# Joined score tiles, softmax steps for two heads at once, and earlier chunk additions in a kernel of attention and MLP

## The chip, the core and the metric

The kernel runs on one core of one Trainium2 chip. The metric is the device time of one execution in microseconds (us); lower is better. Three runs of the kernel before gave 613.06, 613.56 (the median) and 614.54 us. The profile shown here is of another execution, which took 613.01 us.

A core has these engines: TensorE (PE, matrix products; its weight loads are listed as PEld), VectorE (DVE, elementwise arithmetic), ScalarE (ACT, activation functions and copies), GpSimd (POOL), and SyncE (SP), which here only issues DMAs. Each has its own queue of instructions and runs it in order. They wait for each other with semaphores.

## The reference

Causal attention over 4 batches of 12 heads, 448 tokens and 64 features a head, and behind it an MLP on the 1792 tokens with 768 features, 2048 hidden features and a leaky ReLU:

```
scores = scale * q @ k.T                 # per batch and head, 448 x 448
scores = where(mask, -1e9, scores)       # mask: triu(k=1), causal
scores = scores - max(scores, axis=-1)
attn   = exp(scores); attn = attn / (sum(attn, axis=-1) + 1e-9)
x      = attn @ v                        # heads side by side: 1792 x 768
h      = x @ w_in                        # 768 x 2048
out    = maximum(0.01 * h, h) @ w_out    # 2048 x 768
```

q, k and v are float32. The two weight matrices come as float64 and are read as pairs of 32-bit words.

## The kernel before

**Units.** Two heads of one batch make a unit; there are 24, u = 0 to 23, six to a batch. A unit's scores lie with the keys on the 128 partitions and the queries on the columns, in four chunks of 128 keys. Since the mask is causal, chunk c needs only the queries from 128c on: 448, 320, 192 and 64 columns. Chunks 3 and 0 of a head fill one PSUM bank, chunks 2 and 1 a second, so a unit takes four banks. Four banks have the names S0 to S3; up to unit 7 the two banks of layer 1 (mm0, mm1) serve as well, so that a unit and a half have room.

**Steps of a unit** (lines of before):
- `features`: PE transposes k and q (L375), ACT copies them out (kq, L378).
- `scores`: 16 matmuls (L404) and eight small ones that add the mask (L418); in the text "S".
- `head`, for each of the two heads: ACT copies chunk 0 into M (L433); DVE takes the maximum of M and chunks 1, 2, 3, three instructions (L435 to 437, shown by the profile at the helper's line L236); POOL reduces M over the partitions (L438, result MR); DVE subtracts MR from the chunks, four instructions of 64, 448, 192 and 320 columns into t (L443); ACT takes exp of t (L450).
- `products`: 16 matmuls t by v (L462), which ACT copies out as xu (L468).
- `finish`, after each second unit: PE sums t over the keys for four heads with a matrix of ones (L482). In batches 0 and 1 all four chunks are summed, 32 matmuls. In batches 2 and 3 DVE first adds the chunks onto each other (`add`, L488 to 492, three instructions a head) and PE sums one chunk, 8 matmuls. ACT copies the sums out (sr, L494); a DMA spreads them, DVE takes the reciprocal (L497, L498), DMAs store and broadcast it (rb), DVE divides (L512), and x is split into a rounded part (x hi, ACT, L513) and the rest (x lo, DVE, L514).

**Weights.** `weights_in` unpacks w_in in 16 pieces: one ACT and three DVE instructions make a float32 of the words (L316 to L322), ACT rounds it into wh (L337), DVE takes the rest, wl (L340). The stage tile for it shares its memory with x of batches 1 and 3.

**MLP.** `layer1` multiplies x by a piece for one batch: 18 matmuls make one h tile (L536), 64 tiles, 1152 matmuls. ACT applies the leaky ReLU (L542) and SP writes the tile to DRAM. `weights_out` and `layer2` follow, with 1176 matmuls at L723.

**What sets the order.** `Plan` collects the instructions with a planned duration and a due time, and then lists them one by one: the engine that is free first takes, of its instructions that are ready at that time by the plan, the one with the smallest due time (L105 to 109). A step's due time is the unit's number plus an entry of the table LATER (`turn`, L207). The pieces of weights have PIECE[0] + PIECE[1] * f (L746), layer 1 numbers far behind (L767 to 769), so its matmuls fill what attention leaves free; SAME favours a PE instruction of the same kind as the last. The list is then the program order on every engine; on the chip, an engine waits in that order.

**Memory.** M and MR have two tiles each, t six (NTB), one per head.

Of the kernel before, what the change touches and what calls it, by code (L numbers as in the profile page):

```python
# [8 lines left out]
F32 = mybir.dt.float32  # L9
# [11 lines left out]
    "add": 89.39, "load": -27.59, "v": 46.78, "transpose": 57.39, "features": 318.14, "scores": 12.88,  # L21
    "chunk 0": 37.99, "max": -23.03, "all max": -55.97, "subtract": -12.57, "exp": 18.88, "products": 35.62,
    "take products": 0, "sums": -9.93, "take sums": -52.68, "spread": -20.75, "invert": 56.94, "store": -44.79,
    "broadcast": 373.59, "divide": 13.16, "x hi": -28.06, "x lo": 62.49,
}

EARLY = 8

PIECE = (97.36, -5.57)


SAME = 25.68
# [115 lines left out]
def attention_moe_kernel(  # L148
# [52 lines left out]
    for j in range(2):  # L201
        P.slot["mm", ("S", 4 + j)] = j
# [51 lines left out]
    place = p1.tile([128, S], F32, tag="M0", name="place")[:, 0:128]  # L254
# [9 lines left out]

    big = [pp.tile([128, 512], F32, tag=f"big{i}", name="big") for i in range(2)]
# [6 lines left out]
    memset(lambda: place[:, 0:1], 0.0, (), [("M", 0)], FIRST)  # L272
    for i in range(7):
        n = 2 ** i
        dve(n, lambda n=n: nc.vector.tensor_scalar(out=place[:, n:2 * n], in0=place[:, 0:n], scalar1=float(n), scalar2=None, op0=ALU.add),
            (), [("M", 0)], FIRST)
    pe(0.3, lambda: nc.tensor.matmul(out=at_row, lhsT=place[0:1, :], rhs=ones[0:1, 0:1], start=True, stop=True), [("M", 0), "ones"], ["at_row"], FIRST)
    dve(1, lambda: nc.vector.tensor_copy(out=row, in_=at_row), ["at_row"], ["row"], FIRST)
    def table(out_, n, col, key, **how):
        dve(n, lambda: nc.vector.tensor_scalar(out=out_, in0=place[:, 0:n], scalar1=col, **how), ["row", "rows", ("M", 0)], [key], FIRST)  # L280
# [102 lines left out]
    order = sorted(segs)  # L383

    def scores(u):

        kq = ("kq", u % 2)


        sl = [2 * ((2 * u + bank) % 3 if u < EARLY else bank) + e for e in range(2) for bank in range(2)]  # L390
        S_ = ("S", u)

        def f(banks):
            for bank in banks:
                for e in range(2):
                    j = sl[2 * e + bank]
                    T[S_, 2 * e + bank] = (mm if j > 3 else pp).tile([128, 512], F32, tag=f"mm{j - 4}" if j > 3 else f"S{j}", name="S")
            for bank in banks:
                cs = [c for c in order if segs[c][2] == bank]
                for c in cs:  # L400
                    qs, n, _, col = segs[c]
                    for e in range(2):
                        rows = slice(64 * e, 64 * e + 64)
                        nc.tensor.matmul(out=T[S_, 2 * e + bank][:, col:col + n], lhsT=T[kq][rows, 128 * c:128 * c + 128],  # L404
                                         rhs=T[kq][rows, S + qs:2 * S], start=c == cs[0], stop=False)

            for i, w in enumerate((first, last_)):
                for bank in banks:
                    for e in range(2):
                        rows = slice(64 * e, 64 * e + 64)  # L410
                        o = T[S_, 2 * e + bank]
# [8 lines left out]
        for banks in ((0,), (1,)) if u <= EARLY else ((0, 1),):  # L420
            pe(1.17 * len(banks), lambda banks=banks: f(banks), [kq, (*kq, 0), (*kq, 1), "maskb"], [("S", sl[2 * e + bank]) for bank in banks for e in range(2)],
               turn("scores", u), rows=120, cfg=1)
        for e in range(2):
            head(2 * u + e, e, sl)

    def head(g, e, sl):

        u = g // 2
        S_ = ("S", u)
        m, mr, t = ("M", g % 2), ("MR", g % 2), ("t", g % NTB)  # L430
        bk = lambda c: ("S", sl[2 * e + segs[c][2]])
        s = lambda c: T[S_, 2 * e + segs[c][2]][:, segs[c][3]:segs[c][3] + segs[c][1]]
        act(S + 55, both(new(m, p1, [128, S], F32, f"M{g % 2}"), lambda: nc.scalar.activation(out=T[m], in_=s(0), func=ACTF.Copy)),  # L433
            (), [m, bk(0)], turn("chunk 0", u))
        for c in order[1:]:  # L435
            qs, n, _, _ = segs[c]
            tt(lambda qs=qs: T[m][:, qs:], lambda c=c: s(c), lambda qs=qs: T[m][:, qs:], ALU.max, n, (), [m, bk(c)], turn("max", u), chain=0.02)
# [369 lines left out]
```

## Time and profile before

| | |
|---|---|
| median of 3 runs | 613.56 us (613.06 to 614.54) |
| profiled execution | 613.01 us, of which the span of the trace is 611.1 us |
| PE busy | 597.0 us, 98% of the span |
| DVE busy | 446.9 us, 73% |
| ACT busy | 292.1 us, 48% |
| POOL busy | 82.2 us, 13% |
| TensorE clock granted | 1.00, the upper of its two levels (2.4 GHz) |

"Busy" counts the time in which an engine executes. In a timeline, neighbouring instructions of one kind are drawn together with their count (x4), and the text names the shape of the first; the time in brackets at the end is idle time in front of the row, with the engine whose signal ended it. A shape 128x448 is partitions by columns. The steps of weights and attention fill the trace up to 263 us; the last quarter of layer 1 and layer 2 follow.

### The profile page before, as it was taken

Reading aid. Unit: us, or ns where it says so; the run is one execution under the profiler, and the core shown is the slowest. Engines: PE = TensorE matmul, PEld = TensorE weight load, DVE = VectorE, ACT = ScalarE, POOL = GpSimd, SP = SyncE. Lnnn points to the kernel's source line nnn. Section 1 sums busy time; section 2 is a strip of 40 time slices with the busy share of each in tenths; the row PEclk is TensorE's granted clock in tenths of the full one; section 3 lists DMA queues with packets and bytes.
Section 4 is the critical chain, followed back from the end, with each engine's and each line's share of the span. In section 5 each row is a group of like instructions: output and inputs, shape, how many; then the busy total and the mean of one; then the engine's idle time right before and its main releaser. Section 6 shows DMA issues by size and latency. Waiting matters only on the chain.

```text
span 611.1 us, 10491 instructions
## 1 busy us (share of the span) xinstructions
PE 597.0 (98%) x3850; PEld 517.7 (85%) x3850; DVE 446.9 (73%) x935; ACT 292.1 (48%) x499; POOL 82.2 (13%) x54
## 2 busy tenths in 40 slices
PE   8889999999999999999999999999999999999997
PEld 6656666779867677789999999999999999999997
DVE  3899998999579778711466799778857676767655
ACT  3767766666555554512333555545333233323231
POOL 1545332332024234200000000000000000000000
PEclk9999999999999999999999999999999999999999
DMA  8987977855474433112588764113523333333201
GB/s 166 240 175 158 194 195 165 240 166 164 124 165 113 118 106 81 43 57 88 196 274 276 276 209 131 62 47 103 156 70 121 89 117 110 99 95 96 70 30 39
DMA packets 130466, 82.90 MB, mean 136 GB/s; under 512 B 72560, under 2 KB 128368, under 8 KB 130416
## 3 DMA queue, kind: packets, MB, share of 16 engines
q1 hardware_dynamic: 126576, 76.74, 44.6%
q10 hardware_dynamic: 3840, 5.51, 3.4%
q8 instruction: 30, 0.49, 0.3%
q14 instruction: 20, 0.16, 0.1%
HBM read 61.87 MB, written 20.27 MB: 134 GB/s over the span
## 4 chain that ended last, share of the span: by engine, by line
PE 74%; DVE 14%; DMA 4%; issue 3%; ACT 3%; POOL 3%; SPq 0%; ACTq 0%; POOLq 0%; DVEq 0%
PE h L723 31%; PE h L536 30%; PE S L404 4%; PE big L462 4%; DVE t L443 3%; DVE M L236 3%; POOL MR L438 3%; PE big L375 2%; PE big L482 2%; DMA rb<-scr 1%; DVE wl L340 1%; DVE stage L319 1%; DVE stage L321 1%; DMA stage<-in_moe_w_in_dram 1%; DMA kraw<-in_k_dram 1%
## 5 line engine op out<-in xcount | busy, mean ns | idle before, releaser
L536 PE MATMUL h<-xt,wh 128*128 128x448 f32 x768 | 222.7, 371 | 0.0
L723 PE MATMUL h<-W,r 128*128 128x384 f32 x882 | 164.1, 334 | 0.1
L723 PEld LDWEIGHTS h<-W,r 128*128 128x128 f32 x882 | 153.7, 188 | 0.7 <-DVE r L589 0.4
L536 PEld LDWEIGHTS h<-xt,wh 128*128 128x128 f32 x768 | 141.6, 188 | 13.8 <-issue 0.7
L536 PE MATMUL h<-xt,wl 128*128 128x448 f32 x384 | 140.9, 367 | 0.0
L438 POOL PARTITION_ALL_REDUCE MR<-M x48 | 81.7, 1747 | 171.5 <-DVE M L236 136.8
L536 PEld LDWEIGHTS h<-xt,wl 128*128 128x128 f32 x384 | 72.1, 188 | 6.7
L588 ACT ACTIVATE r<-v 128x512 fp32r<-128x512 f32 x70 | 41.9, 599 | 71.8 <-DVE v L586 71.7
L542 ACT ACTIVATE h<-h 128x448 f32<-128x448 f32 x64 | 34.7, 542 | 76.6 <-PE h L536 49.6
L443 DVE TENSOR_TENSOR t<-S,MR 128x64 f32<-128x64 f32 x192 | 67.5, 413 | 4.9 <-POOL MR L438 4.7
L589 DVE TENSOR_TENSOR r<-v,r 128x512 fp32r<-128x512 f32 x70 | 47.3, 690 | 28.4 <-ACT r L588 26.6
L236 DVE TENSOR_TENSOR M<-S,M 128x320 f32<-128x320 f32 x144 | 49.1, 354 | 20.7 <-ACT M L433 9.6
L723 PE MATMUL h<-xw,r 128*128 128x384 f32 x294 | 61.9, 334 | 0.0
L450 ACT ACTIVATE t<-t 128x1024 f32<-128x1024 f32 x48 | 50.7, 1057 | 21.2 <-DVE t L443 17.0
L404 PE MATMUL S<-kq 64*128 64x448 f32 (+3 forms) x384 | 57.0, 412 | 0.1
L723 PEld LDWEIGHTS h<-xw,r 128*128 128x128 f32 x294 | 51.9, 188 | 0.0
L404 PEld LDWEIGHTS S<-kq 64*128 64x128 f32 x384 | 36.1, 191 | 18.7 <-issue 13.4
L586 DVE TENSOR_TENSOR v<-A 128x512 f32<-128x512 f32 (+1 forms) x71 | 47.7, 689 | 0.0
L462 PE MATMUL big<-t,v 128*64 128x448 f32 (+3 forms) x384 | 46.6, 386 | 0.1
L462 PEld LDWEIGHTS big<-t,v 128*64 128x64 f32 x384 | 25.4, 136 | 21.9 <-issue 11.4
L433 ACT ACTIVATE M<-S 128x448 f32<-128x448 f32 x48 | 24.3, 539 | 23.4 <-POOL MR L438 11.8
L588 ACT ACTIVATE r<-A 128x512 fp32r<-128x512 f32 x28 | 17.7, 632 | 30.8 <-PE h L723 30.7
(84 smaller groups left out, 525.4 us busy)
## 6 DMA issues: line engine op xcount, KB each, us to landing
gd<-h SPq DMA_DIRECT2D x64, 224.0 KB, 2.3
A<-gd SPq DMA_DIRECT2D x28, 512.0 KB, 3.7
stage<-in_moe_w_in_dram SPq DMA_DIRECT2D x16, 768.0 KB, 5.8
A<-in_moe_w_out_dram SPq DMA_DIRECT2D x16, 768.0 KB, 5.7
kraw<-in_k_dram SPq DMA_DIRECT2D x24, 224.0 KB, 3.8
qraw<-in_q_dram SPq DMA_DIRECT2D x24, 224.0 KB, 4.3
rb<-scr ACTq DMA_DIRECT2D x48, 112.0 KB, 3.1
v<-in_v_dram SPq DMA_DIRECT2D x48, 96.0 KB, 3.2
```

Source lines behind the costliest of these rows:

```text
L236: return dve(n, lambda: nc.vector.tensor_tensor(out=out_(), in0=a(), in1=b(), op=op), r, w, prio, **kw)
L404: nc.tensor.matmul(out=T[S_, 2 * e + bank][:, col:col + n], lhsT=T[kq][rows, 128 * c:128 * c + 128], rhs=T[kq][rows, S + qs:2 * S], start= ...
L438: P.op("Pool", 1.75, both(new(mr, p1, [128, S], F32, f"MR{g % 2}"), lambda: nc.gpsimd.partition_all_reduce(T[mr], T[m], 128, ReduceOp.max) ...
L443: f = lambda c=c, qs=qs, n=n: nc.vector.tensor_tensor(out=T[t][:, at(c):at(c) + n], in0=s(c), in1=T[mr][:, qs:], op=ALU.subtract)
L450: act(1024 + 55, lambda: nc.scalar.activation(out=T[t], in_=T[t], func=ACTF.Exp, scale=scale), (), [t], turn("exp", u))
L462: nc.tensor.matmul(out=bigs(key[1])[64 * e:64 * e + 64, qs:S], lhsT=T[vv][:, c, e, :], rhs=T["t", (2 * u + e) % NTB][:, 512 * bank + col:5 ...
L536: nc.tensor.matmul(out=T[key][:, :S], lhsT=T[w, f, 1][:, 128 * c:128 * c + 128], rhs=T["xt", b][:, x, :], start=(c == 0 and j == 0), stop= ...
L542: lambda key=key, g=g: nc.scalar.activation(out=T[g], in_=T[key][:, :S], func=ACTF.Prelu, alpha=0.01)),
L586: nc.vector.tensor_tensor(out=x(), in0=get(terms[0]), in1=get(terms[1]), op=ALU.add if terms[2] > 0 else ALU.subtract)
L588: act(n, lambda: nc.scalar.activation(out=hi(), in_=x(), func=ACTF.Copy), [*rd, *hold], [(out_cell, "h")], prio)
L589: return dve(n, lambda: nc.vector.tensor_tensor(out=lo(), in0=x(), in1=hi().bitcast(F32), op=ALU.subtract), [*rd, (out_cell, "h")], [out_c ...
L723: nc.tensor.matmul(out=T[key][:, :HO], lhsT=g()[:, jj * 128:jj * 128 + 128], rhs=W[:, w * HO:(w + 1) * HO], start=(e == 0 and jj == 0 and ...
```

## The change

Five things are changed:

1. A unit's score banks are joined in pairs: the two heads' banks of one kind make one tile of two banks, [128, 2, 512]. There are two such tiles, SS, apart from layer 1's two banks, which serve as the third pair up to unit 7.
2. M, MR and t become tiles for both heads, with two tiles of M, one of MR and three of t. MR and t keep their size so, and M's memory doubles.
3. One instruction may then do a step for both heads. The copy of chunk 0 does so wherever the bank pair is a joined tile (all units but 1, 4 and 7); maxima and subtractions do so from unit 8, the ninth, on. The all-reduce stays one for each head, and so does exp.
4. Chunk additions (and so 8 matmuls of sums in place of 32) begin at batch 1 instead of batch 2, each instruction for both heads of a unit.
5. The tables LATER, PIECE and SAME have new numbers, and the all-reduce's planned duration is 1.52 instead of 1.75. The constants at the start use rb0's memory instead of M0's.

```diff
 LATER = {
-    "add": 89.39, "load": -27.59, "v": 46.78, "transpose": 57.39, "features": 318.14, "scores": 12.88,
+    "add": 62.28, "load": -49.69, "v": 26.95, "transpose": 115.6, "features": -54.79, "scores": -10.32,
...
-PIECE = (97.36, -5.57)
+PIECE = (260.59, -34.81)
-SAME = 25.68
+SAME = -28.38
...
+    SS = [pp.tile([128, 2, 512], F32, tag=f"S{i}", name="S") for i in range(2)]
...
+    NTB, NM = 3, 2
+    ADDS = 1
+    MERGE = [lambda u: u >= 0, lambda u: u >= 8, lambda u: u >= 8]
+    for tag, n, width_ in (("M", NM, S), ("MR", 1, S), ("t", NTB, 1024)):
+        for i in range(n):
+            T[tag, i] = p1.tile([128, 2, width_], F32, name=f"{tag}{i}")
...
-        sl = [2 * ((2 * u + bank) % 3 if u < EARLY else bank) + e for e in range(2) for bank in range(2)]
+        sl = [(2 * u + bank) % 3 if u < EARLY else bank for bank in range(2)]
...
+                    T["S", u, bank, e] = SS[sl[bank]][:, e] if sl[bank] < 2 else mm.tile([128, 512], F32, tag=f"mm{e}", name="S")
...
+        heads = lambda merged: [(0, 1)] if merged else [(0,), (1,)]
...
+        for es in heads(MERGE[0](u) and sl[0] < 2):
+            act(len(es) * S + 55, lambda es=es: nc.scalar.activation(out=T[m][:, cut(es)], in_=s(0, es), func=ACTF.Copy),
+                (), cells(m, es) + bk(0, es), turn("chunk 0", u))
+        for es in heads(MERGE[1](u) and max(sl) < 2):
+            for c in order[1:]:
+                qs, n, _, _ = segs[c]
+                tt(lambda qs=qs, es=es: T[m][:, cut(es), qs:], lambda c=c, es=es: s(c, es), lambda qs=qs, es=es: T[m][:, cut(es), qs:], ALU.max, len(es) * n,
+                   (), cells(m, es) + bk(c, es), turn("max", u), chain=0.02)
         for e in range(2):
...
+            P.op("Pool", 1.52, lambda e=e: nc.gpsimd.partition_all_reduce(T[mr][:, e], T[m][:, e], 128, ReduceOp.max),
+                 [(*m, e)], [(*mr, e)], turn("all max", u))
...
+        for es in heads(MERGE[2](u) and max(sl) < 2):
+            for c in (3, 0, 2, 1):
+                qs, n, bank, col = segs[c]
+                i = dve(len(es) * n, lambda c=c, qs=qs, n=n, es=es: nc.vector.tensor_tensor(
+                    out=T[t][:, cut(es), at(c):at(c) + n], in0=s(c, es), in1=T[mr][:, cut(es), qs:], op=ALU.subtract),
+                    cells(mr, es), cells(t, es) + bk(c, es), turn("subtract", u))
...
+        for e in range(2):
+            act(1024 + 55, lambda e=e: nc.scalar.activation(out=T[t][:, e], in_=T[t][:, e], func=ACTF.Exp, scale=scale), (), [(*t, e)], turn("exp", u))
...
-        chunks = order[:1] if b >= 2 else order
-        for g in heads if b >= 2 else ():
+        chunks = order[:1] if b >= ADDS else order
+        for w in (u - 1, u) if b >= ADDS else ():
...
-                tt(lambda at=at, c=c: at(c, 128), lambda at=at, c=c: at(c, 128), lambda at=at, c=c: at(c + 1, 0), ALU.add, n,
-                   (), [("t", g % NTB)], turn("add", u), chain=0.02)
+                tt(lambda at=at, c=c: at(c, 128), lambda at=at, c=c: at(c, 128), lambda at=at, c=c: at(c + 1, 0), ALU.add, 2 * n,
+                   (), [("t", w % NTB, e) for e in range(2)], turn("add", u), chain=0.02)
```

How the tables and the merging move instructions is seen in the program order at two places.

DVE of before, around the last conversions of weights; M is unit 14's maxima (of head after head), wl the rest of a piece of weights, t<-S unit 14's first subtractions:

```order
L340 TENSOR_TENSOR wl_1_1747<-stage,wh_1_1739 128x768
L236 TENSOR_TENSOR M_1745<-S,M_1745 128x320
L236 TENSOR_TENSOR M_1745<-S,M_1745 128x192
L236 TENSOR_TENSOR M_1745<-S,M_1745 128x64
L236 TENSOR_TENSOR M_1749<-S,M_1749 128x320
L236 TENSOR_TENSOR M_1749<-S,M_1749 128x192
L236 TENSOR_TENSOR M_1749<-S,M_1749 128x64
L340 TENSOR_TENSOR wl_1_1778<-stage,wh_1_1679 128x768
L443 TENSOR_TENSOR t_1784<-S,MR_1767 128x64
L443 TENSOR_TENSOR t_1784<-S,MR_1767 128x448
```

DVE of after, around the last conversions; t_102 is unit 13's subtraction, stage and wl belong to the weights, xt to x lo of batch 1, M_98 is unit 14's maxima:

```order
L456 TENSOR_TENSOR t_102<-S,MR_100 128x2x448
L318 TENSOR_SCALAR stage<-stage 128x768
L320 SCALAR_TENSOR_TENSOR stage<-stage 128x768
L322 SCALAR_TENSOR_TENSOR stage<-stage 128x768
L341 TENSOR_TENSOR wl_1_1662<-stage,wh_1_1638 128x768
L456 TENSOR_TENSOR t_102<-S,MR_100 128x2x192
L341 TENSOR_TENSOR wl_1_1674<-stage,wh_1_1667 128x768
L456 TENSOR_TENSOR t_102<-S,MR_100 128x2x320
L236 TENSOR_TENSOR xt_1683<-rb_213,xt_1683 128x448
L236 TENSOR_TENSOR xt_1683<-rb_123,xt_1683 128x448
L236 TENSOR_TENSOR M_98<-S,M_98 128x2x320
L236 TENSOR_TENSOR M_98<-S,M_98 128x2x192
```

In before, unit 13 is done at this place and unit 14's maxima and subtractions stand between the conversions. In after, unit 13's four merged subtractions are spread over the last conversions, the last of them behind the last wl, and unit 14 begins behind x lo.

PE of before behind unit 16's scores; S<-maskb are the last matmuls of the scores, h is layer 1, big<-t,v unit 15's products:

```order
L418 MATMUL S<-maskb,last 128x2x64
L418 LDWEIGHTS last
L418 MATMUL S<-maskb,last 128x2x64
L536 MATMUL h<-xt_1917,wh_1_474 128x448 x2
L536 MATMUL h<-xt_1917,wl_1_688 128x448
L536 MATMUL h<-xt_1917,wh_1_474 128x448 x2
L536 MATMUL h<-xt_1917,wl_1_688 128x448
L536 MATMUL h<-xt_1917,wh_1_474 128x448 x2
L536 MATMUL h<-xt_1917,wl_1_688 128x448
L462 MATMUL big<-t_2132,v_95 64x448
L462 MATMUL big<-t_2149,v_95 64x448
```

PE of after behind unit 16's scores, with the same names; big<-ident is a block of transposes:

```order
L421 MATMUL S<-maskb,last 128x2x64
L421 LDWEIGHTS last
L421 MATMUL S<-maskb,last 128x2x64
L474 MATMUL big<-t_101,v_97 64x448 x2
L474 MATMUL big<-t_101,v_97 64x320 x2
L474 MATMUL big<-t_101,v_97 64x192 x2
L474 MATMUL big<-t_101,v_97 64x64 x2
L376 MATMUL big<-ident,qraw_93 128x112 x4
L548 MATMUL h<-xt_1683,wh_1_520 128x448 x2
L548 MATMUL h<-xt_1683,wl_1_620 128x448
```

In before, nine layer-1 matmuls stand between unit 16's scores and unit 15's products. In after the products come straight behind the scores, and the layer-1 matmuls follow.

## Rows read from the trace of the kernel before

**Rows 1.** The page: busy time of each engine; the chain that ended last.
```profile
PE 597.0 (98%) x3850; PEld 517.7 (85%) x3850; DVE 446.9 (73%) x935; ACT 292.1 (48%) x499; POOL 82.2 (13%) x54
...
PE 74%; DVE 14%; DMA 4%; issue 3%; ACT 3%; POOL 3%; SPq 0%; ACTq 0%; POOLq 0%; DVEq 0%
```

**Rows 2.** Windows by stage: length; busy PE, PEld, DVE, ACT, POOL; granted clock.
```profile
70.00:137.20 67.20, 63.63 (x512) 46.45 (x510) 62.31 (x130) 45.50 (x69) 21.28 (x12) 1.00 0.76 193
137.20:163.20 26.00, 25.80 (x129) 23.57 (x126) 21.48 (x44) 14.39 (x22) 3.21 (x2) 1.00 0.42 133
163.20:263.00 99.80, 99.78 (x733) 72.49 (x733) 77.20 (x222) 54.28 (x91) 29.52 (x18) 1.00 0.42 108
263.00:400.60 137.60, 137.60 (x666) 124.98 (x667) 84.44 (x138) 57.11 (x107) 0.00 (x0) 1.00 0.52 174
```

**Rows 3.** Windows: the stretch with weight conversions, columns as before.
```profile
19.00:157.30 138.30, 130.21 (x1052) 96.14 (x1049) 130.35 (x293) 95.31 (x148) 48.96 (x28) 1.00 0.74 180
```

**Rows 4.** Timeline of PE, row sums: start, us, operation, count, idle before.
```profile
120.40 1.93 PE L482 MATMUL big<-t,ones 128*32 128x448 f32 x32 [0.47 <-ACT kq L378]
...
174.76 1.68 PE L482 MATMUL big<-t,ones 128*32 128x448 f32 x8
...
212.73 0.96 PE L482 MATMUL big<-t,ones 128*32 128x448 f32 x8
```

**Rows 5.** DVE groups by form, subtractions: count, busy us, mean ns, idle before.
```profile
L443 DVE TENSOR_TENSOR t<-S,MR 128x448 f32<-128x448 f32 x48 | 29.4, 612 | 0.0
...
L443 DVE TENSOR_TENSOR t<-S,MR 128x64 f32<-128x64 f32 x48 | 10.4, 217 | 4.9 <-POOL MR L438 4.7
```

**Rows 6.** Timeline of DVE near the last conversions, and additions later.
```profile
134.06 1.40 DVE L443 TENSOR_TENSOR t<-S,MR 128x64 f32<-128x64 f32 x4
...
139.69 2.18 DVE L236 TENSOR_TENSOR M<-S,M 128x320 f32<-128x320 f32 x6
...
155.25 0.95 DVE L340 TENSOR_TENSOR wl<-stage,wh 128x768 fp32r<-128x768 f32 x1
...
213.76 1.13 DVE L236 TENSOR_TENSOR t<-t 128x64 f32<-128x64 f32 x3
```

**Rows 7.** Windows of L536 alone: layer-1 matmuls counted behind PE's busy time.
```profile
0.00:137.18 137.18, 30.48 (x135) 24.44 (x135) 1.00 0.81 189
137.18:159.60 22.42, 22.41 (x111) 20.77 (x112) 1.00 0.40 129
```

**Rows 8.** Timeline, all engines: one unit's cycle.
```profile
208.62 2.11 PE L404 MATMUL S<-kq 64*128 64x448 f32 x16
...
208.76 1.02 ACT L233 ACTIVATE xt<-rb 128x448 fp32r<-128x448 f32 x2
...
210.96 0.98 ACT L433 ACTIVATE M<-S 128x448 f32<-128x448 f32 x2 [0.74 <-PE S L418]
...
212.96 3.40 POOL L438 PARTITION_ALL_REDUCE MR<-M  x2 [6.65 <-DVE M L236]
...
216.39 1.42 DVE L443 TENSOR_TENSOR t<-S,MR 128x64 f32<-128x64 f32 x4
...
217.84 1.06 ACT L450 ACTIVATE t<-t 128x1024 f32<-128x1024 f32 x1
...
218.01 2.11 PE L404 MATMUL S<-kq 64*128 64x448 f32 x16
```

**Rows 9.** Timeline of POOL: pairs of all-reduces, beside conversions and later.
```profile
20.66 3.80 POOL L438 PARTITION_ALL_REDUCE MR<-M  x2 [3.77 <-DVE M L236]
...
203.12 3.19 POOL L438 PARTITION_ALL_REDUCE MR<-M  x2 [5.92 <-ACT kq L378]
```

**Rows 10.** Timeline of PE: waits inside attention, the releaser in brackets.
```profile
88.60 0.60 PE L375 MATMUL big<-ident,qraw 112*128 112x112 f32 x4 [1.06 <-ACT xu L468]
...
98.44 1.93 PE L482 MATMUL big<-t,ones 128*32 128x448 f32 x32 [1.31 <-ACT kq L378]
...
163.22 0.60 PE L375 MATMUL big<-ident,kraw 112*128 112x112 f32 x4 [0.22 <-ACT xu L468]
```

More of the change, by code (lines that the diff above doesn't have):

```diff
@@ L20 @@
 LATER = {
-    "add": 89.39, "load": -27.59, "v": 46.78, "transpose": 57.39, "features": 318.14, "scores": 12.88,
-    "chunk 0": 37.99, "max": -23.03, "all max": -55.97, "subtract": -12.57, "exp": 18.88, "products": 35.62,
-    "take products": 0, "sums": -9.93, "take sums": -52.68, "spread": -20.75, "invert": 56.94, "store": -44.79,
-    "broadcast": 373.59, "divide": 13.16, "x hi": -28.06, "x lo": 62.49,
+    "add": 62.28, "load": -49.69, "v": 26.95, "transpose": 115.6, "features": -54.79, "scores": -10.32,
+    "chunk 0": -68.51, "max": -125.69, "all max": -52.02, "subtract": -54.84, "exp": -3.77, "products": -46.61,
+    "take products": -44.44, "sums": -87.48, "take sums": -7.04, "spread": 22.17, "invert": -68.92, "store": 51.82,
+    "broadcast": -0.61, "divide": 2.78, "x hi": -63.62, "x lo": -47.02,
 }
 EARLY = 8
-PIECE = (97.36, -5.57)
-SAME = 25.68
+PIECE = (260.59, -34.81)
+SAME = -28.38
 class Plan:
@@ L420, in scores @@
         for banks in ((0,), (1,)) if u <= EARLY else ((0, 1),):
-            pe(1.17 * len(banks), lambda banks=banks: f(banks), [kq, (*kq, 0), (*kq, 1), "maskb"], [("S", sl[2 * e + bank]) for bank in banks for e in range(2)],
+            pe(1.17 * len(banks), lambda banks=banks: f(banks), [kq, (*kq, 0), (*kq, 1), "maskb"], [("S", sl[bank], e) for bank in banks for e in range(2)],
                turn("scores", u), rows=120, cfg=1)
-        for e in range(2):
-            head(2 * u + e, e, sl)
@@ L426, in head @@
[L426 to L437, printed above, removed]
-        P.op("Pool", 1.75, both(new(mr, p1, [128, S], F32, f"MR{g % 2}"), lambda: nc.gpsimd.partition_all_reduce(
-            T[mr], T[m], 128, ReduceOp.max)), [m], [mr], turn("all max", u))
-        at = lambda c: 512 * segs[c][2] + segs[c][3]
-        for c in (3, 0, 2, 1):
-            qs, n, bank, col = segs[c]
-            f = lambda c=c, qs=qs, n=n: nc.vector.tensor_tensor(out=T[t][:, at(c):at(c) + n], in0=s(c), in1=T[mr][:, qs:], op=ALU.subtract)
-            if c == 3:
-                f = both(new(t, p1, [128, 1024], F32, "t%d" % t[1]), f)
-            last = max(n for n in range(2 * EARLY) if n % 3 == 2)
-            gives = ("mm", ("S", sl[2 * e + bank])) if 2 * u + bank == last and c in (0, 1) else None
-            dve(n, f, [mr], [t, bk(c)], turn("subtract", u), give=gives)
-        act(1024 + 55, lambda: nc.scalar.activation(out=T[t], in_=T[t], func=ACTF.Exp, scale=scale), (), [t], turn("exp", u))
```

46 lines of the change are left out of this document (29 added, 17 removed).

## The prediction

> **What bounds the kernel now.** I read the page's shares first. TensorE (PE) is busy for 98% of the span and makes up 74% of the chain that ended last, with DVE at 14% [rows 1]. So only two things count: matmul time that goes away, and time in which PE stands still. The windows say where it stands still: PE is busy for 63.63 of 67.20 us up to 137.2, but for 25.80 of 26.00, 99.78 of 99.80 and 137.60 of 137.60 in the three stretches behind that, at a granted clock of 1.00 throughout [rows 2]. DVE is busy for 130.35 of 138.30 us between 19 and 157.3 [rows 3]: in the first quarter DVE, which unpacks the w_in weights and does the softmax arithmetic, paces the rest, and PE fills up with layer-1 matmuls (h) only as far as weights are ready. From 137 us to the end of attention (262) PE is the bound and DVE has room.
>
> **What PE loses.** Row sums by 32 matmuls take 1.93 us, by 8 matmuls 0.96 [rows 4]. With chunk additions from batch 1 on, the sums at units 7, 9 and 11 shrink: 3 x 0.97 = 2.9 us. No other PE instruction goes or comes; the order changes.
>
> **What DVE gains and pays.** A merged instruction saves one start. From the two subtraction rows, 612 - 217 = 395 ns for 384 columns is 1.03 ns a column [rows 5]. Four subtractions of one head hold 1024 columns, 1.055 us, and take 1.42 [rows 8]: 0.09 each for starting, of which 0.07 hold up the next. For both heads merged I take 2.46 (2.11 for the columns, four starts), four starts fewer than two such rows: 0.27 less. Six maxima hold 1152 columns, 1.19, and take 2.18 [rows 6]: 0.165 each, three starts fewer, 0.47 less and 1.71 left. Three additions of one head take 1.13 [rows 6] for 576 columns (0.59): 0.18 each, so a merged unit takes 1.62 start to start, where two heads took 2.10. Nearest bounds for the merged forms: nothing saved (two separate rows), or all of 0.151 us (217 less 64 x 1.03) per instruction removed.
>
> Now the DVE work ahead of the last weight conversion, which starts at 155.25 in before [rows 6]:
> - unit 14's maxima and subtractions move behind it (the order excerpt shows it): 2.1 + 2.6 = 4.7 less;
> - units 8 to 13 are merged, 6 x (0.47 + 0.27) = 4.4 less;
> - two heads' additions of batch 2 move behind it, 2.1 less;
> - the additions of units 6 to 12 are now ahead of it, 7 x 1.62 = 11.3 more.
> The sum is +0.1: the weights become ready at 156.2, as before. But unit 13's subtractions, which ended at about 135.5 [rows 6], are now strewn between the last conversions, the last of them behind the last weight; with 640 columns and a start, 0.73 us, it ends at 156.9. I add 0.4 for the merged copy in the early units (a head's maxima wait for both heads) and 0.8 for unit 6, where nothing stands between maxima and subtractions any more: 158, between 155 (none of it, all starts saved) and 160 (each all-reduce beside conversions takes 3.80 instead of 3.19 [rows 9]). S of unit 14 can't finish before that: its fifth matmul overwrites what the last subtraction reads, and the remaining matmuls are 1.6 us. End of S(14): 159.6.
>
> PE has 252 h matmuls ahead of that point; before had done 135 + 111 = 246 by 159.6 [rows 7]. Six at 137.60 / 666 = 0.207 [rows 2] are 1.2 us, and one block of transposes more (0.4) is done: 1.6 us ahead. By its work alone PE would be there at 137.2 + 117 x 0.207 - 2.9 = 158.5, so the subtraction costs it 1.1 of the 2.9. With DVE at either bound the lead is 2.7 or -0.4.
>
> **The stretch after 160.** In before a unit repeats every 9.4 to 9.8 us: S at 208.62 and 218.01 [rows 8]. The path inside it: S 2.34 to the copy's start, two copies 0.98, maxima of one head (0.16 after the first copy), two all-reduces 3.40, subtractions 1.42, and the second head's work runs beside the first's: the second subtraction ends at 217.81, S follows at 218.01 and exp at 217.84. Merged, both heads go in step: S 2.34 + copy 0.94 + hop 0.16 + maxima 1.71 + hop 0.17 + two all-reduces 3.3 + the first two subtractions 1.2 + hop 0.2 = 10.05 to the next S. Both exps (2.1 us) now start only when the last merged subtraction ends, and they stand ahead of the next copy on ACT: S would let the copy start 1.3 us after the subtractions, the exps let it at 2.1, so the cycle is up to 10.9. PE's own content per unit in the new order, from rows (S 2.24, products 1.88, 24 to 30 h, sums in every other unit, two blocks of transposes) is 11.0 to 11.9. So the chain mostly hides behind PE, by 0.1 to 1 us, where before had nothing to hide. Where work that waits stands in between, PE will stand still. Following the new orders of DVE, ACT and PE with these durations I find:
> - products 13: their PSUM bank is given free by a copy behind an x-hi copy (half of 1.02 [rows 8]) that waits for unit 9's division behind unit 14's maxima: 1.45;
> - S of units 16 and 18, one behind additions and a reciprocal fed by a DMA, one behind additions: 0.6 and 0.4;
> - products 15, directly behind S(16) (excerpt), wait for the second exp: 2.1 + 0.2 after the last subtraction, against S's end at 1.3: 1.0;
> - products 19 (the reciprocal stands between the subtractions) 0.7, sums 21 (additions behind unit 22's maxima and a division) 0.9, products 22 0.4.
> Together 5.45. Against it stand before's own waits that go: sums that took 1.68 instead of 0.96 at 174.76 [rows 4] and 0.22 at 163.22 [rows 10], 0.9 together. Bounds for the new waits: 1 (only the largest stays) and 11 (next part). POOL's planned time and the other tables act through the order alone. From layer 1's last two batches on, the order of all engines is the same as before, so a shift there reaches the end unchanged; 600 h are left after attention where 678 were.
>
> **Sum.** Profiled execution 613.01 (span 611.1 and 1.9 around it; 0.55 under the median of 613.56): -1.6 - 0.9 + 5.45 = +2.95, so 616.0; its own range, with 155 to 160 for DVE and 3 to 8 us of waits, 612.5 to 619.5.
>
> **A rule that would speak against it.** Additions ran at 213.76 for 1.13 us inside the all-reduces of 212.96 [rows 6, 8]; the sum of their own means is 1.09, and the pair took 3.40 where one without additions took 3.19 [rows 9]: 0.2 us on POOL's side, no stop. The Trainium skill, "SBUF — State Buffer", section "SBUF: two separate sides", says that a DVE operation with two SBUF inputs and a GpSimd operation that reads SBUF exclude each other through a shared port pair, and the later one fully blocks. By that rule each of the seven addition units ahead of the last weight could wait for an all-reduce. As a mechanism of this kernel, a stop would last one all-reduce of up to 1.7 us (half of 3.40), 7 x 1.7 = 11.9, and the time about 628. The trace disagrees with it for these shapes.
>
> **Rivals.**
> *PE simply keeps what it gets (faster).* DVE's starts are saved in full, unit 13 ends at 156, and the new waits don't come because PE's content per unit exceeds the chain. For it: 10.05 to 10.9 against 11.0 to 11.9. Against: the waits above aren't waits for the chain but for the order on ACT and DVE. 613.01 - 2.9 - 0.9 = 609.2; if PE's waits in the first part (1.06 at 88.60, 1.31 at 98.44 [rows 10]) also go, 606.8.
> *The merged chain paces every unit (slower).* If one unit of additions (1.62) falls between all-reduce and subtraction, or ahead of the maxima, in each cycle, the cycle is 10.9 + 1.6 = 12.5 against a mean content of about 11.3, 9 x 1.2 = 10.8 from S(15) to S(23): 613.01 - 1.6 - 0.9 + 10.8 = 621.3. It decides once a cycle passes PE's content. For it: DVE does 8 of 11 us a unit there. Against: all-reduces leave 3.3 us in which additions fit.
> *Gain and waits cancel.* Only the waits at products 13 and 15, 2.45: 613.0. The merging then shortens DVE, which has room there, and does nothing for time.
> *The port stops additions*, above: 628.
>
> **Chances.** Forecast 0.40, PE keeps its gain 0.30, no net change 0.12, chain paces 0.16, port 0.02. What a measurement of this kernel can tell from no change is 0.3%, 1.8 us: 611.7 to 615.4. Of the forecast's 0.40, 0.26 lie above and 0.14 within; of the gain's 0.30, 0.28 below; of the cancelling's 0.12, 0.04 below. Faster 0.32, same 0.24, slower 0.44. Range 607 to 622: it takes in nearly all of the gain's case and half of the pacing one's.
>
> **What the changed profile would show.** The last weight's conversion near 156 and unit 13's last subtraction near 157 to 158 (under 156: the gain's case). Merged subtractions of four at 2.4 to 2.5, maxima of three at 1.6 to 1.7; sums of 8 matmuls at units 7, 9, 11. S of units 15 to 23 about 11.3 us apart, with PE waits of 0.4 to 1.5 before products 13, 15, 19 and sums 21; PE busy 594 and the waits behind 160 about 5 us. It is wrong if PE is fed between 160 and 265 as before, if S repeats in under 10.5 or over 12 us, or if the weights are ready 3 us earlier or later.

## The result: slower, by more than forecast

| | before | changed |
|---|---|---|
| median, six runs each (lowest to highest) | 613.30 us (610.92 to 614.54) | 618.23 us (617.19 to 621.11) |
| ratio, 95% interval | | 1.0091 (1.0072 to 1.0110) |
| profiled execution, span of its trace | 613.01, 611.1 us | 617.98, 616.2 us |

The forecast was 616.0, a loss of 2.4 us against the median known then and 3.0 against the profiled execution; the loss is 4.9 by the medians and 5.0 by the two profiled executions. The direction was right and the time lies in the forecast's range, but the loss is 1.7 to 2 times the forecast's.

The page of the changed kernel, busy time of each engine, answers to [rows 1]; the windows of the same stretches answer to [rows 2] (length, then busy PE, PEld, DVE, ACT, POOL with counts, granted clock):

```profile
PE 594.1 (96%) x3744; PEld 514.3 (83%) x3744; DVE 458.8 (74%) x805; ACT 290.3 (47%) x478; POOL 83.7 (14%) x54
```

```profile
70.00:137.20 67.20, 62.26 (x420) 46.30 (x417) 65.86 (x95) 39.83 (x59) 17.47 (x10) 1.00 0.69 179
137.20:163.20 26.00, 24.25 (x132) 19.73 (x132) 25.34 (x36) 13.61 (x21) 3.98 (x2) 1.00 0.57 176
163.20:263.00 99.80, 97.45 (x684) 73.36 (x681) 69.47 (x116) 52.56 (x82) 28.83 (x17) 1.00 0.44 110
```

PE's work is 2.9 us less, as worked out, with 106 instructions fewer. But PE stands still for 1.8 us between 137 and 163, where it stood 0.2 before, and for 2.4 us behind that, where it stood next to none. DVE executes 130 instructions fewer in the whole and is busy 11.9 us longer. That last pair is the riddle: the merged instructions cost what was forecast (below), so something makes instructions long. TensorE's clock is not it: from 70 us on the granted clock is 1.00 in both kernels, and ahead of that it fell only once, to 0.83 on average between 10 and 20 us in the changed kernel.

The timeline of PE in the changed kernel at unit 14's scores (start, us, operation, count, idle before with its releaser), the place that the forecast put at 159.6:

```profile
160.72 1.19 PE L407 MATMUL S<-kq 64*128 64x448 f32 x8
162.73 1.14 PE L407 MATMUL S<-kq 64*128 64x320 f32 x8 [0.81 <-DVE t L456]
163.69 0.28 PE L421 MATMUL S<-maskb,first 64*128 64x128 bf16 x4
...
172.26 1.95 PE L474 MATMUL big<-t,v 128*64 128x448 f32 x16 [1.92 <-ACT xu L480]
```

The first eight of the 16 matmuls go early, and the ninth waits for unit 13's last subtraction, as described (the prediction calls it the fifth, since the program writes eight and the trace shows 16); but that subtraction ends near 162.7, and S(14) at 163.99. DVE's timeline ahead of it:

```profile
100.89 1.57 DVE L320 SCALAR_TENSOR_TENSOR stage<-stage 128x768 int32<-128x768 int32 x1
...
111.31 1.74 DVE L236 TENSOR_TENSOR M<-S,M 128x640 f32<-128x640 f32 x3
112.97 2.48 DVE L236 TENSOR_TENSOR t<-t 128x128 f32<-128x128 f32 x3
115.37 1.69 DVE L341 TENSOR_TENSOR wl<-stage,wh 128x768 fp32r<-128x768 f32 x1
116.98 2.47 DVE L456 TENSOR_TENSOR t<-S,MR 128x128 f32<-128x128 f32 x4
...
135.07 1.74 DVE L236 TENSOR_TENSOR t<-t 128x128 f32<-128x128 f32 x3
...
160.99 0.95 DVE L341 TENSOR_TENSOR wl<-stage,wh 128x768 fp32r<-128x768 f32 x1
161.85 0.82 DVE L456 TENSOR_TENSOR t<-S,MR 128x640 f32<-128x640 f32 x1
```

Merged maxima take 1.74 and merged subtractions 2.47 (forecast 1.71 and 2.46). But the same three additions take 1.74 at 135.07 and 2.48 at 112.97, the same wl 0.95 at 160.99 and 1.69 at 115.37, and the conversion at 100.89, elsewhere 0.96, takes 1.57. POOL's rows say what else ran (x2 is a pair; its second all-reduce begins 1.5 to 1.6 us behind its first):

```profile
100.58 3.34 POOL L450 PARTITION_ALL_REDUCE MR<-M  x2 [9.81 <-DVE M L236]
113.24 3.67 POOL L450 PARTITION_ALL_REDUCE MR<-M  x2 [9.31 <-DVE t L236]
```

Each long one began shortly behind an all-reduce's start, or holds an instruction that did. I call the extra time a hold: the time of an instruction above that of its form's short ones, counted from 0.2 us on. DVE's time up to the end of the last weight or of unit 13's last subtraction, whichever is later, then splits, from all its rows, into idle time (gaps of over 0.15 us), holds, and clean work from start to start (the last instruction's own time comes on top):

| kernel | end | idle | holds | clean work |
|---|---|---|---|---|
| before | 156.2 | 14.5 | 1.7 (3 of them) | 139.1 |
| changed | 162.7 | 11.9 | 9.6 (15) | 140.3 |

Clean work grew by 1.2, holds by 7.9, idle time fell by 2.6. From the start of layer 2 on (first matmul 403.14 before, 408.22 now) both kernels take 208.0 us, so the whole loss arises ahead of it.

### The profile page after: what moved, and what is told of

Read it like the earlier page. It is cut to its first block, busy times and chain, and to the rows that moved or that the text cites. A ratio compares the mean times of both kernels' runs of the same rounds, so it can differ in the third digit from the quotient of the medians.

```text
span 616.2 us, 10011 instructions
## 1 busy us (share of the span) xinstructions
PE 594.1 (96%) x3744; PEld 514.3 (83%) x3744; DVE 458.8 (74%) x805; ACT 290.3 (47%) x478; POOL 83.7 (14%) x54
## 4 chain that ended last, share of the span: by engine, by line
PE 69%; DVE 16%; ACT 4%; DMA 4%; issue 3%; POOL 2%; ACTq 1%; SPq 0%; DVEq 0%; POOLq 0%
PE h L735 31%; PE h L548 27%; PE big L474 4%; PE S L407 4%; DVE t L456 4%; POOL MR L450 2%; DVE M L236 2%; DVE wl L341 2%; PE big L376 2%; DVE stage L320 1%; DMA stage<-in_moe_w_in_dram 1%; DVE stage L322 1%; DMA rb<-scr 1%; PE big L494 1%; DVE t L236 1%
## 5 line engine op out<-in xcount | busy, mean ns | idle before, releaser
L548 PE MATMUL h<-xt,wh 128*128 128x448 f32 x768 | 222.1, 370 | 0.0
L548 PEld LDWEIGHTS h<-xt,wh 128*128 128x128 f32 x768 | 141.1, 188 | 14.3 <-issue 2.9
L548 PE MATMUL h<-xt,wl 128*128 128x448 f32 x384 | 140.5, 366 | 1.6 <-DVE wl L341 1.6
L450 POOL PARTITION_ALL_REDUCE MR<-M x48 | 83.2, 1782 | 192.8 <-DVE M L236 121.2
L548 PEld LDWEIGHTS h<-xt,wl 128*128 128x128 f32 x384 | 72.1, 188 | 8.1 <-DVE wl L341 2.3
L456 DVE TENSOR_TENSOR t<-S,MR 128x64 f32<-128x64 f32 (+7 forms) x128 | 62.5, 547 | 6.5 <-POOL MR L450 6.4
L236 DVE TENSOR_TENSOR M<-S,M 128x320 f32<-128x320 f32 (+5 forms) x96 | 43.1, 456 | 30.4 <-ACT M L442 21.2
L407 PE MATMUL S<-kq 64*128 64x192 f32 (+3 forms) x384 | 54.2, 406 | 6.3 <-DVE t L456 6.1
L407 PEld LDWEIGHTS S<-kq 64*128 64x128 f32 x384 | 33.2, 187 | 26.2 <-issue 12.4
L474 PE MATMUL big<-t,v 128*64 128x320 f32 (+3 forms) x384 | 50.3, 386 | 3.5 <-ACT xu L480 2.1
L474 PEld LDWEIGHTS big<-t,v 128*64 128x64 f32 x384 | 28.4, 136 | 28.5 <-issue 10.4
L236 DVE TENSOR_TENSOR t<-t 128x128 f32<-128x128 f32 (+2 forms) x54 | 39.7, 734 | 9.7 <-PE big L474 8.6
```

What stands on the lines that cost most here:

```text
L236: return dve(n, lambda: nc.vector.tensor_tensor(out=out_(), in0=a(), in1=b(), op=op), r, w, prio, **kw)
L407: nc.tensor.matmul(out=T["S", u, bank, e][:, col:col + n], lhsT=T[kq][rows, 128 * c:128 * c + 128], rhs=T[kq][rows, S + qs:2 * S], start=c ...
L450: P.op("Pool", 1.52, lambda e=e: nc.gpsimd.partition_all_reduce(T[mr][:, e], T[m][:, e], 128, ReduceOp.max), [(*m, e)], [(*mr, e)], turn(" ...
L456: i = dve(len(es) * n, lambda c=c, qs=qs, n=n, es=es: nc.vector.tensor_tensor(out=T[t][:, cut(es), at(c):at(c) + n], in0=s(c, es), in1=T[m ...
L474: nc.tensor.matmul(out=bigs(key[1])[64 * e:64 * e + 64, qs:S], lhsT=T[vv][:, c, e, :], rhs=T["t", u % NTB][:, e, 512 * bank + col:512 * ba ...
L548: nc.tensor.matmul(out=T[key][:, :S], lhsT=T[w, f, 1][:, 128 * c:128 * c + 128], rhs=T["xt", b][:, x, :], start=(c == 0 and j == 0), stop= ...
```

## The experiments

All edits below but two keep the program order of the changed kernel, or of before, on PE, ACT, POOL and SP, and touch single DVE instructions alone (late_reduce also moves each unit's first all-reduce back); adds_from_2 and merge_only are planned anew. The edits are shortened to what changes in the order of the instructions. Each ratio is to runs of before taken beside the variant, with medians from 611.95 to 612.90 us.

**split_max.** The changed kernel with the merged maxima written per head:

```diff
-  M[both], chunk 1; M[both], chunk 2; M[both], chunk 3
+  M[0], chunk 1; M[0], chunk 2; M[0], chunk 3; M[1], chunk 1; M[1], chunk 2; M[1], chunk 3
```

> The changed kernel with its order kept; only the merged maxima of units 8 to 23 are written as one instruction a head (head 0 first), so that the first all-reduce can start while head 1's maxima, which read PSUM, still run. Theory (held at the all-reduce): DVE instructions that read SBUF and start in the first 0.6 us of an all-reduce are held 0.55 to 0.78 us, 20 us in sum up to 300 us in the changed kernel against 4 in before; with the split about half of the holds go (to 8 to 12 us), which outweighs the 0.47 us of starts a unit: unit 13's last subtraction about 159 to 161 instead of 161.85, time 614.5 to 617.5. Rival (what counts is the number of DVE starts): no hold depends on it, DVE has 6 x 0.47 = 2.8 us more ahead of unit 13's last subtraction (near 164.5), time 619 to 622.

Measured: unit 13's last subtraction at 160.9, holds ahead of it 4.8 instead of 9.6, clean work 143.2, 2.9 more (forecast 6 x 0.47 = 2.8). The trace at the place shown above, DVE and then POOL:

```profile
109.97 2.18 DVE L447 TENSOR_TENSOR M<-S,M 128x320 f32<-128x320 f32 x6
112.07 2.43 DVE L236 TENSOR_TENSOR t<-t 128x128 f32<-128x128 f32 x3
114.42 0.95 DVE L341 TENSOR_TENSOR wl<-stage,wh 128x768 fp32r<-128x768 f32 x1
...
111.30 3.19 POOL L455 PARTITION_ALL_REDUCE MR<-M  x2 [8.71 <-DVE M L447]
```

The first all-reduce now starts inside the maxima, and the pair takes 3.19 instead of 3.67; the additions begin 0.77 behind its start and are still long, because the third of them meets the start of the second all-reduce; wl is short. So DVE does more and is done sooner: the holds are shown, and the count of starts is refuted as the cause. The median is 617.57 (1.0088 of before, 1.0064 to 1.0111), hardly better than the changed kernel, though PE follows DVE: by 163.99 it has done 261 layer-1 matmuls instead of 253, and the last 600 begin 2.4 us sooner (284.1 against 286.5). Where that went stands in the last section.

**late_reduce.** Before, with the maxima alternating between the heads, and the first all-reduce behind them all:

```diff
-  head 0: 320, 192, 64; all-reduce 0; head 1: 320, 192, 64; all-reduce 1
+  320 of 0 and 1; 192 of 0 and 1; 64 of 0 and 1; all-reduce 0; all-reduce 1
```

> The kernel before with its order kept; only the six maxima of a unit alternate between the heads, and the first all-reduce comes when both heads are done, some 0.8 us later. DVE's work is the same to the instruction. Theory (held at the all-reduce): the instruction behind the maxima now starts together with the first all-reduce and is held 0.7 us where it reads SBUF, 6 to 12 units ahead of the last weight: holds up to 300 us grow from 4 us to 12 to 18, the last weight comes 4 to 9 us later than 155.25, time 616 to 621. Rival (chain length only): the all-reduce pair ends 0.8 us later in each unit and DVE does other work meanwhile, last weight within 1 us of 155.25, time 613 to 615.

Measured: 623.77 us (1.0190, 1.0169 to 1.0212), last weight at 168.25. The time is beyond the theory's range, and for another reason: holds are 3.9, only 2.2 more. DVE's waits up to the last weight, 168.3 and 156.2 (in total, times, longest), the first row of each kernel's list that names POOL, late_reduce and then before:

```profile
DVE t L462 <- POOL MR L449: 16.4, 18, 1.8
```

```profile
DVE t L443 <- POOL MR L438: 2.2, 9, 0.8
```

Subtractions wait 14.2 us more for the all-reduce, since in this order little stands between. So this run shows the price of a late all-reduce, not of holds, and supports neither theory as written. It showed something else: the alternating maxima keep DVE busy for 25.5 us up to there instead of 30.7. I put that down to none of them waiting for its own predecessor, which no run isolates.

**cover.** The changed kernel, with a needless copy out of PSUM behind the merged maxima:

```diff
   nc.vector.tensor_tensor(out=M[both], in0=chunk 3, in1=M[both], op=ALU.max)
+  nc.vector.tensor_copy(out=T["M", (u + 1) % NM][:, :, :], in_=s(0, (0, 1)))
```

> The changed kernel with its order kept; behind the merged maxima of units 8 to 23 DVE copies both heads' chunk 0 once more from PSUM into the idle M tile (896 columns, about 1.0 us, nothing reads it). Theory (DVE instructions that read SBUF are held when they start in an all-reduce's first 0.6 us): the copy reads PSUM alone and runs over that time, so the holds at the first all-reduce of units 8 to 13 (0.6 to 0.75 each, 4.1 us) go; six copies cost 6.0: unit 13's last subtraction at about 164.6 instead of 162.67, holds up to there near 5.5 instead of 9.6. Rival (the long instructions are slow for another reason, say the weights' DMAs): holds stay near 9.6 and the subtraction comes at about 168.7. Time 619 to 621 by the theory, 623 to 626 by the rival.

Measured: holds 4.5 instead of 9.6 (the theory said near 5.5); unit 13's last subtraction at 166.3 (6.8 us more clean work, copies and all, and 2.0 more idle time), between the two forecasts. The time, 626.76 us (1.0215, 1.0182 to 1.0248), is above both ranges; ten more copies stand behind that place, and the long run of layer-1 matmuls went at the slower of the two paces of the last section. Unit 10's stretch, DVE and then POOL, where the changed kernel had the conversion of 1.57:

```profile
100.87 1.08 DVE L451 COPY M<-S 128x896 f32<-128x896 f32 x1
101.86 0.62 DVE L318 TENSOR_SCALAR stage<-stage 128x768 int32<-128x768 int32 x1
102.52 0.96 DVE L320 SCALAR_TENSOR_TENSOR stage<-stage 128x768 int32<-128x768 int32 x1
103.40 1.61 DVE L236 TENSOR_TENSOR t<-t 128x128 f32<-128x128 f32 x2
...
101.14 3.80 POOL L454 PARTITION_ALL_REDUCE MR<-M  x2 [10.71 <-DVE M L236]
```

An instruction that reads PSUM runs over the all-reduce's start and is not held (1.08 with its neighbours), and the conversions behind it have their short times. The additions at 103.40 meet the second all-reduce and are long. A cause in the weights' DMAs would have left the holds at 9.6.

**no_additions_b1.** The changed kernel without the additions of batch 1:

```diff
   tt(at(c, 128), at(c, 128), at(c + 1, 0), ALU.add, 2 * n, ...)
+  if b == 1: emit nothing in its place
```

> The changed kernel with its order kept; the 18 additions of batch 1 are left out, so the row sums of batch 1 are wrong, and PE still sums 8 matmuls. It prices the additions. Clean work of 6 x 1.62 = 9.7 us goes and the holds on them (2.2). If DVE's sum is what sets unit 14's scores, the last subtraction of unit 13 comes at 151 to 153 instead of 162.67, PE becomes the bound there (158) and the time is 611.5 to 614. If the new waits behind 160 were the larger part of the loss, S of unit 14 moves as said, and the time stays above 616.

Measured: 616.89 us (1.0057, 1.0038 to 1.0076). Clean work falls by 8.7 and holds by 3.6, but idle time rises by 8.5, 4.7 of it before subtractions: the additions filled waits for the all-reduce. Unit 13's last subtraction comes at 158.9, not 151 to 153. My pricing of the additions at their full length was wrong here: they cost 3.8 us at that place, not 12. PE again follows (271 layer-1 matmuls by 163.99, 18 more), but layer 2 begins only 1.4 us sooner (406.9 against 408.2), because the long run went at the slower pace, which costs 2.4.

**adds_from_2 and merge_only.** Additions from batch 2 on, with the changed kernel's tables; and beside that the tables of before:

```diff
-    ADDS = 1
+    ADDS = 2
```

> The changed kernel with additions from batch 2 on (sums of 32 matmuls at units 7, 9 and 11 again), its tables and merging kept; the order is planned anew. DVE has six units of additions less in batch 1 (6 x 1.62 = 9.7 us and their holds, about 3), PE 2.9 us more. If the additions with their holds are what moved the last weights, unit 13's last subtraction comes 6 to 12 us earlier than 161.85 and the time is 612 to 616; if the tables or the merging are, it stays within 3 us and the time is 617 to 621.

> Joined tiles and merged steps as in the changed kernel, but additions only from batch 2 as in before, and the tables LATER, PIECE, SAME and the all-reduce's planned 1.75 of before. It tells the merging from the additions and the tables. Theory (held at the all-reduce): merging saves 0.74 us a unit on DVE and gives about as much back in holds, so the last weight stays near 155 to 157 and the time at 612 to 616. Rival (additions in batch 1 are the whole price): merging alone brings 6 x 0.74 = 4.4 us of DVE ahead of the last weight, weights at about 151, time 609 to 612.

Measured: 622.89 us (1.0183, 1.0148 to 1.0219) and 632.27 (1.0330, 1.0305 to 1.0356). Both are slower than the changed kernel and above all their forecasts, with 22.7 and 21.5 us of idle DVE time ahead of unit 13's last subtraction against 11.9. That subtraction ends at 163.6 and 162.0, against 162.7 in the changed kernel; in merge_only the last weight is ready at 145.1, 11 us sooner than in before, and it does not help. My reading is that tables that fit one set of steps leave holes with another; in merge_only the granted clock also fell for stretches, to 0.95 on average up to 164 us (0.99 in the changed kernel). So neither run prices its part; only that merging with the old tables is worse than with the new is plain.

**alternate_half and split_alternate.** Since alternating maxima are cheaper, the same in a form that keeps the first all-reduce early; on before, and on split_max:

```diff
-  320, 192, 64 of head 0; 320, 192, 64 of head 1
+  320 of 0; 320 of 1; 192 and 64 of 0; 192 and 64 of 1
```

> The kernel before with its order kept; in each unit the maxima come as head 0's 320, head 1's 320, head 0's 192 and 64, head 1's 192 and 64, instead of three and three, so that two of the four steps that wait for their own predecessor have another between. In late_reduce six alternating maxima took about 1.6 us instead of 2.1. Here 0.24 us a unit should go, and the first all-reduce starts 0.15 later only: 14 units ahead of the last weight, 3.4 us, last weight at 152.5 to 154 instead of 156.2, time 610 to 612.5, faster by 1 to 3 us. If waits for the all-reduce eat it, as in late_reduce, the last weight stays at 156 or later and the time is 613 to 616.

> split_max with the same half alternation in units 8 to 23: one instruction a head, head 0's 320, head 1's 320, head 0's 192 and 64, head 1's 192 and 64. By DVE's sum and the holds: 0.24 us less a unit than split_max, six units, unit 13's last subtraction at 159.5 instead of 160.93 with holds near 5 again, time 1 to 2 us under split_max: 615.5 to 617. If the first all-reduce's start is again behind all maxima's, holds go back to 9 and the subtraction to 162.

Measured: 617.10 (1.0060, 1.0037 to 1.0084) and 620.33 (1.0118, 1.0090 to 1.0146): slower both times, against my forecast. In alternate_half clean work fell by 3.2, near the forecast (3.4), holds rose from 1.7 to 7.8 and idle time by 1.2; the last weight came at 160.4 instead of 156.2. In split_alternate clean work fell by 1.7 and holds rose by 3.2. Two wl of alternate_half, DVE and then POOL:

```profile
110.78 1.93 DVE L438 TENSOR_TENSOR M<-S,M 128x320 f32<-128x320 f32 x6
112.62 1.47 DVE L340 TENSOR_TENSOR wl<-stage,wh 128x768 fp32r<-128x768 f32 x1
...
115.34 0.94 DVE L340 TENSOR_TENSOR wl<-stage,wh 128x768 fp32r<-128x768 f32 x1
...
112.35 3.21 POOL L444 PARTITION_ALL_REDUCE MR<-M  x2 [6.99 <-DVE M L438]
```

The maxima end sooner after the all-reduce's start, the next SBUF instruction begins 0.27 behind it instead of 0.8 or later, and is held 0.53. This is the cleanest case: less DVE work, no other edit, a later end, and 6.1 of the difference in the holds. (Its granted clock was 0.97 on average up to 164 us; what that cost DVE can only be in the 1.2 of idle time.)

**split_both.** split_max, with the subtractions per head as well:

```diff
-  S - MR for both heads: 64, 448, 192, 320 columns a head
+  head 0: 64, 448, 192, 320; head 1: 64, 448; 192; 320
```

> split_max with the merged subtractions of units 8 to 23 written per head as well, head 0's four first, order kept: only the copy of chunk 0 and the additions stay merged. Theory: the waits of the products for exp behind 160 us (1.2, 0.36 and 0.63 us of PE at units 15, 16 and 22 in the changed kernel) come from both exps starting behind both heads' subtractions; split, exp of head 0 starts 1.2 us earlier and these waits fall to under 0.5 in sum; unit 13's last subtraction within 1.5 us of split_max's 160.93; the last row sums at 281 to 283 against 283.6 in split_max, time 615 to 617. If these waits have another cause they stay at 2 us, and DVE's extra starts (0.27 a unit) make it 618 to 619.

Measured: 619.28 (1.0103, 1.0059 to 1.0147). Behind unit 16's scores, products 15 now follow without a wait (the first of these rows of PE), and products 16 behind unit 17's with 0.3 (the second, 2.24 against 1.95):

```profile
190.65 1.95 PE L483 MATMUL big<-t,v 128*64 128x448 f32 x16
...
201.80 2.24 PE L483 MATMUL big<-t,v 128*64 128x448 f32 x16
```

The waits for exp fall from 2.2 to 0.3 us, so they came from both exps starting behind merged subtractions. But unit 13's last subtraction came at 163.4, 2.5 later than in split_max: 1.9 more clean work, 0.6 more holds, 0.3 more idle, and a last instruction shorter by 0.3. The time follows that place.

**after_again and before_again.** Both kernels unaltered:

> The changed kernel once more, unaltered, for the spread of what the marks show: unit 13's last subtraction at 162 to 163.5, holds ahead of it 9 to 10 us. In its first trace the long run of layer-1 matmuls behind attention went at 202.7 ns a matmul, in before's at 206.7; if that is set by the execution and not by the kernel, it may now be 206.7, and the time 620 to 621.

> The kernel before once more, unaltered: last weight at 155 to 157.5, holds ahead of it 1.5 to 3 us. If the pace of the long run of layer-1 matmuls is set by the execution, it may be 202.7 ns instead of 206.7, and the time then 610 to 611.

Measured: 617.66 and 613.51 us; ends at 162.2 and 156.8, holds 8.5 and 0.9 (both a little under what I expected), clean work 140.3 and 139.0. The accounting repeats to 1.1 us in the holds and 1.4 in idle time. The pace of the long run did not change with the execution (last section).

No variant beats before.

## Why the prediction was wrong, step by step

- *What PE loses*: right. PE is busy 594.1, forecast 594; the sums take 0.96.
- *DVE's clean work*: right. The ledger, +0.1 to the last weight and 0.73 for the last subtraction, is +1.1 in the trace; merged rows take 1.74 and 2.47; the last weight and unit 13's subtractions lie strewn as the order said. The bounds on the merged forms were not the trouble.
- *The step that failed* is the sentence "0.2 us on POOL's side, no stop", and with it the end of unit 13 at 158. I had read one row: additions at 213.76 inside an all-reduce that began at 212.96 [rows 6, 8]. They start 0.80 us behind its start, just when the hold is over, and I took the one for all. In before, maxima of the second head, which read PSUM, fill that time in nearly every unit; merging them removes this cover. The maxima around the all-reduce of 203.12 [rows 9] are the first of the rows of before under this step; they end 0.88 behind its start. The second and third are one of before's three holds, a conversion that takes 0.55 elsewhere, and its all-reduce: the trace of before had the sign. The 3.80 of [rows 9], which I used as a bound alone, was the same contention seen from POOL. The mechanism to which I gave 0.02 was there: 15 holds instead of before's 3, in additions, conversions and wl alike, most of 0.5 to 0.8 us, where the rival's price was seven of 1.7 in additions alone. It adds 7.9 us; unit 13 ends 4.7 later than forecast, mainly because idle time fell by 2.6, as holds fill waits, where I had added 0.4 and 0.8. S(14) ends at 163.99 instead of 159.6.

```profile
201.81 2.19 DVE L236 TENSOR_TENSOR M<-S,M 128x320 f32<-128x320 f32 x6 [2.00 <-ACT M L433]
...
118.95 1.33 DVE L317 TENSOR_SCALAR stage<-stage 128x768 int32<-128x768 int32 x1 [0.18 <-DMA stage<-in_moe_w_in_dram]
...
118.93 1.94 POOL L438 PARTITION_ALL_REDUCE MR<-M  x1 [7.60 <-DVE M L236]
```

- *The lead at that point*: 1.6 us forecast. In place of it, at 163.99 the changed kernel has done 253 layer-1 matmuls and before 263: ten behind, 2.1 us, with PE's other remaining work alike. That is 3.7 of the loss that I missed. That PE follows DVE here is shown by split_max and no_additions_b1: 1.7 and 3.8 us earlier at unit 13, 8 and 18 matmuls more at 163.99. (The forecast's 0.207 for these matmuls is the pace behind 263; between 137 and 160 they went at 22.41 / 111 = 0.202 [rows 7], which makes its 158.5 a 157.9.)
- *The waits behind 160*: the sum was right, 5.45 forecast and about 5.1 found, though not at each place. Products 13 1.9 (1.45), products 15 1.2 (1.0), products 22 0.6 (0.4), sums 21 0.5 (0.9), S(16) 0.2 (0.6), products 16 0.4 (not seen), sums at 197.7 0.2 and products at 215.7 0.1 (not seen), S(18) none (0.4), products 19 none (0.7). split_both shows that products 15 and 22 wait for exp, the reason given for products 15. The row at 172.26 above is products 13's.
- *The sum*: 613.0 + 2.1 (ten matmuls) + 5.1 - 0.9 (waits of before that went) = 619.3; measured 618.0. The changed kernel's layer-1 matmuls behind attention go 2.4 us faster in 600, and 1.1 the other way stays unassigned. That pace is luck: before's trace shows both paces (0.202 above and 0.207 [rows 2]), but not which of them the changed kernel would have there. At before's pace the time would have been about 620.4 and the forecast further off.
- *The rivals*: "PE simply keeps what it gets" fails at S(14). "The merged chain paces every unit" fails too: S of units 17 to 23 follow 11.0 to 12.0 us apart, near the forecast 11.3, with PE fed but for the waits above.

Open: that the additions' removal moves unit 13 by so little is only accounted (idle time takes their place), not tried further; how the tables and the merging share the loss was not separated, since each set of tables fits only its own steps; and no run takes away the holds and leaves the rest as it is, so their share of the time is an account, while that they exist and move the end is shown.

## What to carry to other kernels

Before merging instructions, see what each of them covers: a piece that looks like overhead may be what runs while another engine holds a shared resource. When a trace is used to rule out contention, look at where in the other engine's instruction the overlap begins, and at all overlaps, not at one. In an order this tight an edit that saves 3 us of an engine's work can cost 4, so price starts against the other engine's starts too.

## What the runs showed of the hardware that was not expected

**The hold.** An instruction of DVE that reads SBUF alone (conversions, additions, wl, divisions, x lo, even the tiny ones that add 1e-9 to sc, which took 0.90 instead of 0.16) and starts within 0.6 us behind an all-reduce's start is held, in the simplest case until about 0.8 us behind that start. In the 13 traces, up to 300 us, there are 224 of these, and all were held for more than 0.2 us; only two reciprocals, which have one input, were not. One addition of the changed kernel, with its all-reduce:

```profile
113.28 1.31 DVE L236 TENSOR_TENSOR t<-t 128x384 f32<-128x384 f32 x1
```

```profile
113.24 1.60 POOL L450 PARTITION_ALL_REDUCE MR<-M  x1 [9.31 <-DVE t L236]
```

It starts 0.04 behind and takes 0.75 more than its short form (0.56); the wl of alternate_half starts 0.27 behind and takes 0.53 more. Both could go at 0.79 to 0.80. Maxima and subtractions, which take one operand from PSUM, were not held in any of these traces (484 began in that time), nor was the copy of cover. The other way round, an all-reduce that starts while such a DVE instruction runs is longer. The second of the changed kernel's pair at 113.24 starts inside an addition that runs for another 0.69, and takes 2.16, against 1.60 for the single one above:

```profile
114.75 2.16 POOL L450 PARTITION_ALL_REDUCE MR<-M  x1
```

The wl at 115.37 behind it is then held until 1.36 behind this start. What 213 of the 224 share is that they could go about 0.8 us ahead of the all-reduce's end.

The Trainium skill, "SBUF — State Buffer", section "SBUF: two separate sides", says that DVE in a two-port mode, or with two SBUF inputs beside a GpSimd instruction that reads SBUF, and GpSimd exclude each other, and that the one behind blocks for the whole instruction. The traces agree that they exclude each other, and that instructions with one operand in PSUM are free of it; but the DVE instruction is let go 0.8 us ahead of the end of an all-reduce of 1.60, so here the hold lasts for a part of it.

**Two paces of matmuls.** In the long run of layer-1 matmuls behind attention, at a granted clock of 1.00 throughout, matmuls follow each other at 206.7 ns in some kernels and at 202.7 in others. Windows of their line alone (L536, L548 or L553), 300 to 380 us (length, busy PE and PEld with counts, granted clock): before, before_again, changed, after_again, split_max:

```profile
300.00:380.00 80.00, 80.00 (x389) 72.64 (x388) 1.00 0.74 247
```

```profile
300.00:380.00 80.00, 80.00 (x389) 72.68 (x388) 1.00 0.75 247
```

```profile
300.00:380.00 80.00, 80.00 (x396) 74.14 (x395) 1.00 0.74 253
```

```profile
300.00:380.00 80.00, 80.00 (x397) 74.13 (x396) 1.00 0.77 253
```

```profile
300.00:380.00 80.00, 80.00 (x389) 72.66 (x388) 1.00 0.75 248
```

The slow pace is even, 206 and 207 ns; the fast one repeats 199, 207, 202, 203, 202. The two kernels that were run again showed the same pace in both of their traces here, but the pace belongs to a run of matmuls and not to the kernel as a whole: before goes at 202 ns between 137 and 160 [rows 7]. For 600 matmuls the difference is 2.4 us: the changed kernel has the fast pace, split_max the slow one, which is where split_max's lead of 2.4 us went. By the same window late_reduce, merge_only and alternate_half have the fast one (396 or 397) and all others the slow one (389), so two of these times can differ by 2.4 us for this alone. What sets it was not tried.
